# Attention with normalised queries and keys, then an MLP: later starts of three preparation units and a reordered list of first operations

## The chip, the cores and the metric

The kernel runs on one core of a Trainium2 chip. The metric is the device time of one execution in microseconds. Before the change it is 615.18 us, the median of three runs (614.29 to 615.19). The profiled execution took 614.88 us, and its trace spans 613.1 us; times inside the trace are counted from its start.

## The reference

What is computed, for 8 batches, 12 heads, 448 positions and head size 64 (model width 768, hidden width 3072):

```python
q_n, k_n = (rmsnorm(q, g_q), rmsnorm(k, g_k))
scores = scale * np.matmul(q_n, k_n.transpose(0, 1, 3, 2))
scores = scores - np.max(scores, axis=-1, keepdims=True)
attn = np.exp(scores)
attn = attn / (np.sum(attn, axis=-1, keepdims=True) + 1e-09)
x = np.matmul(attn, v)            # heads side by side: (8, 448, 768)
xn = (x - mu) / np.sqrt(var + 1e-06) * g_ln
out = x + np.maximum(xn @ w_ch1, 0.0) @ w_ch2
```

## The kernel before

**Units and pairs.** Two heads make a pair; there are 48 pairs, six to a batch. The data is prepared in units: units 0 and 1 hold one pair each (pairs 0 and 1), all others two. Batch 0 is units 0 to 3, unit 4 is pairs 6 and 7, unit 5 pairs 8 and 9, unit 6 pairs 10 and 11, unit 7 pairs 12 and 13, unit 8 pairs 14 and 15, unit 9 pairs 16 and 17.

**Preparation.** `pieces` (L188) makes the small operations of a unit, each named by a letter: b takes the buffers, a and c are the squares of keys and queries on ACT (ScalarE), d and e their sums on DVE (VectorE), g the inverse roots on ACT, i the keys times the gains (DVE for units 0 and 1, else POOL), j and k the high and low 16-bit half of the keys (j on ACT or POOL, k on DVE), l the scaled queries on DVE, m a second copy of them, v, w and z the values' casts on POOL. The buffers of a unit, `qn` and `khl`, come from a pool that holds two of each (L86), so that a unit can only start to write when an earlier unit's tile has been read for the last time.

**Transposes.** Up to unit 7 the keys and queries of pair p are transposed on the tensor engine (PE): K p (`trans_k`, L308) and Q p (`trans_q`, L320). From pair 6 on both write the one PSUM tile `tr`, which DVE copies out (L318, L335). From unit 8 on (`DMA_UNIT`) the DMA transposes them: pieces x and y (L253, L265), issued by SP.

**Attention.** S p.i (`scores`, L339) is one product of 128 keys with 448 queries on PE and the exponential of it on ACT; two PSUM buffers `psS` hold the products until ACT has read them. V p.i (`values`, L361) multiplies with the values on PE; after V p.6 DVE divides and writes x (`evac_o`, L387). A pair has seven S and seven V. T p (`stats`, L531) takes statistics for the LayerNorm on DVE.

**LayerNorm and MLP.** For batch 0, A, N0 to N2 (DVE), X0 to X2 (transposes on PE, copied out by ACT, ACT and DVE; X0 and X2 use `tr`) and R (ACT) form the LayerNorm; U0 to U2 (`up_first`, L659) are the first three hidden column blocks of the MLP, one token tile each. M is a small maximum on DVE. The rest of the MLP is `mlp_chunks` (L610): up (L621, followed by a ReLU on ACT) and down (L637), the latter in groups of six products, first for columns 0 to 383 and then for 384 to 767 in batch 0.

**What sets the order.** The first attention, up to the first MLP, follows the list `ORDER` token by token, on all engines. L n loads a unit (SP), G loads the LayerNorm gains, G2 scales them, W n loads a third of the first MLP matrix (POOL's queue). From there on `attention` (L458) makes a list of steps, seven for each pair: step 7p+i holds S p.i, V of the pair before, K of pair p+1 at i = 2 and Q of pair p+1 at i = 4. Into these steps it places the pieces of the units 5 and up: the first ones (b, a, i) at step st, the last of the main pieces at step e, the others evenly between:

```python
st = max(7 * (p - 2 - m) + 2, last + 1, 7 * nb0)
e = max(7 * (p - 2) - 1, st + 5)
st, e = EARLY.get(u, (st, e))
...
at = st + (e - st) * x // (k - 1) if x < k else e + 1 + x - k
```

So `EARLY` overrides start and end for the units named in it. Without it, unit 7 has the steps 58 to 69, unit 8 72 to 83, unit 9 86 to 97. The two halves of the second MLP matrix are loaded with the first pieces of units 6 and 7 (L482, issued by POOL). `run_rest` (L698) interleaves: after each piece of the MLP of batch b it emits as many steps of the attention of batch b+1 as its share of the MLP's cost allows. The steps up to 90 fall into the MLP of batch 0; its last 13 pieces are emitted after them, around the LayerNorm of batch 1. In the list `ORDER` the order on each engine is the one written; in `run_rest` that holds for all engines but DVE, whose order is planned when the program is built.

Of the kernel before, what the change touches and what calls it, by code (L numbers as in the profile page):

```python
# [33 lines left out]


ORDER = """
G b0 a0 c0 L4 L5 i0 j0 e0 k0 gq0 l0 b1 m0 a1 c1 K0 Q0 d0 gk0 S0.0 S0.1 i1 e1 d1 g1 j1 l1 m1 z0
k1 b2 a2 S0.2 d2 c2 S0.3 S0.4 K1 V0.0 e2 i2 S0.5 Q1 g2 l2 S0.6 S1.0 j2 V0.1 S1.1 S1.2 m2 b3
V0.2 a3 V0.3 k2 c3 S1.3 K2 V0.4 S1.4 z2 V0.5 Q2 V0.6 V1.0 S1.5 i3 W0 d3 e3 S1.6 V1.1 V1.2 S2.0
j3 T0 V1.3 S2.1 S2.2 Q3 V1.4 S2.3 K3 S2.4 V1.5 V1.6 S2.5 g3 z3 S2.6 V2.0 S3.0 S3.1 V2.1 k3  # L40
S3.2 b4 V2.2 l3 S3.3 V2.3 m3 S3.4 a4 V2.4 K4 Q4 S3.5 V2.5 V2.6 S3.6 Q5 S4.0 V3.0 S4.1 V3.1
V3.2 d4 i4 K5 W1 c4 W2 V3.3 V3.4 V3.5 V3.6 S4.2 S4.3 V4.0 S4.4 S4.5 V4.1 e4 j4 T1 S4.6 S5.0 k4
g4 V4.2 V4.3 V4.4 V4.5 S5.1 l4 S5.2 S5.3 K6 V4.6 S5.4 z4 m4 b5 V5.0 S5.5 V5.1 G2 L6 V5.2 S5.6
V5.3 V5.4 V5.5 Q6 a5 i5 V5.6 T3 T4 S6.0 S6.1 S6.2 S6.3 T5 S6.4 A V6.0 V6.1 N0 V6.2 N1 V6.3
S6.5 S6.6 V6.4 X0 X1 U0 N2 d5 j5 R X2 K7 Q7 c5 e5 g5 k5 z5 l5 L7 V6.5 U1 U2 M m5 V6.6
""".split()
DMA_UNIT = 8
PE_SET = (DMA_UNIT + 1) % 2
EARLY = {5: (42, 49), 6: (47, 56)}
LN_EXP_SET = 6  # L50
UP_FIRST = 3
REC_LO, REC_HI = 1.0 / 3.0e7, 0.5
# [23 lines left out]
class _Fast:  # L76
# [381 lines left out]
    def attention(self):  # L458
# [3 lines left out]
        for u in range(4, nu):  # L462
            p, m = UNIT_PAIR[u], UNITS[u][2]
# [3 lines that stand above are left out]
            pieces = ["bai", "d", "c", "e", "j", "gv", "k", "l", "m", "w", "x", "y"]  # L467
# [469 lines left out]
```

## Time and profile before

| | value |
|---|---|
| time, median of 3 | 615.18 us (614.29 to 615.19) |
| span of the trace | 613.1 us |
| bytes moved by DMA | 75.29 MB, mean 123 GB/s |
| one exponential (128 x 448, L358) | 635 ns, 336 times |
| one up product (128 x 384 or 512 columns, L621) | 353 ns, 1134 times |
| one down product (L637) | 324 ns, 1368 times |

The profile gives for each engine how long it was busy, and the trace gives each instruction with its start and duration and, in brackets, how long the engine had been idle before it and what released it. A matmul's end is modelled, so neighbouring products overlap on paper; the distance from start to start is the better measure. A wait on several things is put down to the one that came last. "DMA share" is the mean busy share of the 16 DMA engines; in some stretches it exceeds 1. "PEld" is the weight load of the tensor engine, which runs beside its products.

### The profile page before, as it was taken

How to read it: one execution, taken by the hardware profiler on the slowest of the kernel's cores; microseconds unless marked ns; L12 is line 12 of the kernel's file. 1: busy time of each engine (PE TensorE's matmuls, PEld its weight loads, DVE VectorE, ACT ScalarE, POOL GpSimd, SP SyncE). 2: the span in 40 equal slices, each digit the busy share in tenths (PEclk: the TensorE clock that was granted, in tenths of full speed). 3: DMA queues.
4: the chain of work that ended last, by engine and by line, in shares of the span. 5: the costliest groups of instructions: out<-in, count | busy, mean ns of one | idle time of the engine just before them, and what ended most of it. 6: DMA issues, size and time to landing. Idle time of an engine off the chain costs nothing.

```text
span 613.1 us, 11532 instructions
## 1 busy us (share of the span) xinstructions
PE 580.8 (95%) x4500; PEld 346.3 (56%) x4500; DVE 286.8 (47%) x618; ACT 361.4 (59%) x697; POOL 188.2 (31%) x245
## 2 busy tenths in 40 slices
PE   2887999799999999999999999999999999999995
PEld 1555566455566666655566666655566666654564
DVE  5898566633356356643346355642355422440011
ACT  5996986338754498538755398537765377214200
POOL 2852621223452245514453145605322000000000
PEclk9999999899999999999999999999999999999999
DMA  9999999275766477847665496838523330030011
GB/s 193 272 212 207 213 221 189 31 222 134 122 109 128 117 123 150 180 106 144 105 108 141 107 136 151 176 104 151 119 59 87 91 61 2 27 104 0 1 52 56
DMA packets 130861, 75.29 MB, mean 123 GB/s; under 512 B 96656, under 2 KB 121040, under 8 KB 130800
## 3 DMA queue, kind: packets, MB, share of 16 engines
q1 hardware_dynamic: 114048, 45.12, 37.5%
q0 software_dynamic: 16080, 28.94, 21.1%
q8 instruction: 37, 0.61, 0.4%
q10 hardware_dynamic: 672, 0.43, 0.2%
q14 instruction: 24, 0.20, 0.1%
HBM read 52.36 MB, written 11.01 MB: 103 GB/s over the span
## 4 chain that ended last, share of the span: by engine, by line
PE 82%; DVE 2%; DMA 2%; ACT 2%; issue 1%; SPq 1%; DVEq 0%; ACTq 0%
PE psC L637 34%; PE psH L621 33%; PE psS L352 7%; PE oA L381 4%; PE oB L383 2%; PE psS L355 1%; PE psS L356 1%; DMA qkv<-in_k_dram 1%; DMA kU<-khl 1%; ACT E L358 1%; ACT qn L215 0%; DVE qn L67 0%; DVE stat L545 0%; DVE khl L240 0%; ACT khl L215 0%
## 5 line engine op out<-in xcount | busy, mean ns | idle before, releaser
L621 PE MATMUL psH<-xnT,w 128*128 128x512 f16 (+1 forms) x1134 | 241.9, 353 | 0.3 <-ACT hT L671 0.3
L637 PE MATMUL psC<-w,hT 128*128 128x384 f16 (+1 forms) x1368 | 235.6, 324 | 0.0
L358 ACT ACTIVATE E<-psS,rr_all 128x448 f16<-128x448 f32 x336 | 206.9, 635 | 47.8 <-PE psS L352 42.6
L623 ACT ACTIVATE hT<-psH 128x512 f16<-128x512 f32 (+1 forms) x189 | 104.1, 551 | 124.4 <-PE psH L621 121.6
L637 PEld LDWEIGHTS <-hT 128*128 128x128 f16 x1368 | 128.1, 98 | 74.8 <-issue 0.7
L621 PEld LDWEIGHTS <-w 128*128 128x128 f16 x1134 | 102.7, 98 | 81.2 <-issue 0.8
L352 PE MATMUL psS<-qU,kU 128*128 128x448 f16 x288 | 100.9, 358 | 10.9 <-ACT E L358 8.9
L381 PEld LDWEIGHTS <-E 128*128 128x128 f16 x1008 | 70.9, 98 | 51.0 <-issue 7.0
L229 POOL TENSOR_TENSOR qkv<-qkv,gprod 128x896 f32<-128x896 f32 x21 | 43.7, 2079 | 99.4 <-ACT khl L215 60.5
L381 PE MATMUL oA<-v,E 128*128 128x65 f16 x864 | 66.9, 194 | 0.1
L641 DVE SCALAR_TENSOR_TENSOR x<-psC,rs_all,x 128x384 f32<-128x384 f32 x48 | 28.9, 615 | 71.7 <-PE psC L637 71.2
L396 DVE RECIPROCAL rec_all<-oA 128x6 f32<-128x6 f32 x48 | 9.3, 194 | 96.6 <-PE oA L381 96.4
L383 PE MATMUL oB<-v,E 128*128 128x65 f16 x288 | 51.9, 194 | 0.1
L127 POOL DMA_DIRECT2D qkv<-in_k_dram x14 | 11.2, 797 | 129.7 <-ACT E L358 67.9
L218 DVE TENSOR_REDUCE ssq<-khl 128x14 f32<-128x896 f32 (+1 forms) x24 | 25.6, 1065 | 48.7 <-ACT khl L215 48.6
L352 PEld LDWEIGHTS <-kU 128*128 128x128 f16 x288 | 28.3, 99 | 24.6 <-issue 6.2
L218 DVE TENSOR_REDUCE ssq<-qn 128x14 f32<-128x896 f32 (+1 forms) x25 | 26.2, 1047 | 25.1 <-ACT qn L215 25.1
L67 DVE SCALAR_TENSOR_TENSOR qn<-qkv,rq 128x256 f16<-128x256 f32 (+1 forms) x72 | 26.5, 424 | 18.0 <-ACT rq L223 17.9
L383 PEld LDWEIGHTS <-E 128*128 128x128 f16 x336 | 32.5, 97 | 0.3 <-DVE xl L403 0.2
L398 DVE TENSOR_TENSOR x<-oA,rec_all 128x384 f32<-128x384 f32 x48 | 26.8, 558 | 1.5
L545 DVE BATCH_NORM_STATS2 stat<-x 128x6 f32<-128x256 f32 (+1 forms) x75 | 26.3, 405 | 0.7
L240 DVE TENSOR_TENSOR khl<-qkv,khl 128x896 f16<-128x896 f32 x21 | 22.8, 1087 | 7.1 <-ACT khl L237 6.3
(104 smaller groups left out, 446.7 us busy)
## 6 DMA issues: line engine op xcount, KB each, us to landing
out_dram<-x SPq DMA_DIRECT2D x20, 384.0 KB, 2.5
qkv<-in_k_dram POOLq DMA_DIRECT2D x14, 384.0 KB, 3.8
qkv<-in_q_dram POOLq DMA_DIRECT2D x14, 384.0 KB, 5.4
qkv<-in_v_dram POOLq DMA_DIRECT2D x14, 384.0 KB, 6.5
w<-in_moe_w_ch_dram POOLq DMA_DIRECT2D x3, 1536.0 KB, 14.5
w<-in_moe_w_ch_dram POOLq DMA_DIRECT2D x2, 2304.0 KB, 27.0
qkv<-in_k_dram SPq DMA_DIRECT2D x7, 384.0 KB, 5.7
qkv<-in_q_dram SPq DMA_DIRECT2D x7, 384.0 KB, 5.1
```

Of the source, the lines that this page charges most:

```text
L67: nc.vector.scalar_tensor_tensor(out=out, in0=x, scalar=8.0, in1=r.unsqueeze(2).broadcast_to([x.shape[0], g, D]), op0=ALU.mult, op1=ALU.mult)
L218: nc.vector.tensor_reduce(out=c["ssq"][:, n], in_=c["sq", n], axis=AX.X, op=ALU.add)
L229: (nc.vector if u in DVE_KG else nc.gpsimd).tensor_tensor(out=c["t"][1], in0=c["t"][1], in1=sh.gprod.unsqueeze(1).broadcast_to([128, g, D] ...
L352: nc.tensor.matmul(ps[:, 0:S], c["main"][:, ts(i, 128)], q[:, ts(h, S)], start=True, stop=True)
L358: nc.scalar.activation(out=c["E"][:, i], in_=ps[:, 0:S], func=AFT.Exp, scale=self.rr[:, g:g + 1], bias=EXP_BIAS)
L381: nc.tensor.matmul(oA[:, t, cs], E[:, i, ts(t, 128)], rhs, start=(i == 0 and t == 0), stop=(i == 6 and t == 2))
L383: nc.tensor.matmul(oB[:, cs], E[:, i, 320:448], rhs, start=(i == 0), stop=(i == 6))
L398: nc.vector.tensor_tensor(out=x[:, :, 128 * hp:128 * hp + 128].rearrange("p t (e d) -> p t e d", e=2), in0=oA[:, :, :, 0:D], in1=rec[:, 0: ...
L621: nc.tensor.matmul(ps[:, 0:N], sh.w1[:, dc, ts(f, 128)], xnT[:, dc, 0:N], start=(dc == 0), stop=(dc == NDC - 1))
L623: nc.scalar.activation(out=hT[:, f, 0:N], in_=ps[:, 0:N], func=AFT.Relu)
L637: nc.tensor.matmul(ps[:, 0:g[1]], hT[:, f, ts(t, 128)], sh.w2[:, f, cols], start=(f == 0), stop=(f == NFF - 1))
L641: nc.vector.scalar_tensor_tensor(out=x[:, cols], in0=ps[:, 0:g[1]], scalar=self.rs[:, b, t:t + 1], in1=x[:, cols], op0=ALU.mult, op1=ALU.add)
```

## The change

The change touches two constants. In `EARLY`, units 7, 8 and 9 start three steps later and end where they did. In `ORDER`, no operation is added or removed; some change places. It is meant to begin a unit only when the older buffers are no longer read, and to fill waits in the passage from the first attention to the first MLP.

```diff
 ORDER = """
-G b0 a0 c0 L4 L5 i0 j0 e0 k0 gq0 l0 b1 m0 a1 c1 K0 Q0 d0 gk0 S0.0 S0.1 i1 e1 d1 g1 j1 l1 m1 z0
-k1 b2 a2 S0.2 d2 c2 S0.3 S0.4 K1 V0.0 e2 i2 S0.5 Q1 g2 l2 S0.6 S1.0 j2 V0.1 S1.1 S1.2 m2 b3
-V0.2 a3 V0.3 k2 c3 S1.3 K2 V0.4 S1.4 z2 V0.5 Q2 V0.6 V1.0 S1.5 i3 W0 d3 e3 S1.6 V1.1 V1.2 S2.0
+b0 a0 c0 L4 i0 j0 e0 k0 gq0 l0 b1 m0 a1 c1 K0 Q0 d0 G gk0 S0.0 S0.1 d1 e1 L5 i1 g1 j1 l1 k1 m1
+z0 b2 a2 S0.2 d2 c2 S0.3 S0.4 K1 V0.0 e2 i2 S0.5 Q1 g2 l2 S0.6 S1.0 j2 V0.1 S1.1 S1.2 m2 b3
+V0.2 a3 V0.3 k2 c3 S1.3 K2 V0.4 S1.4 z2 V0.5 Q2 S1.5 V0.6 V1.0 i3 W0 d3 e3 S1.6 V1.1 V1.2 S2.0
 j3 T0 V1.3 S2.1 S2.2 Q3 V1.4 S2.3 K3 S2.4 V1.5 V1.6 S2.5 g3 z3 S2.6 V2.0 S3.0 S3.1 V2.1 k3
-S3.2 b4 V2.2 l3 S3.3 V2.3 m3 S3.4 a4 V2.4 K4 Q4 S3.5 V2.5 V2.6 S3.6 Q5 S4.0 V3.0 S4.1 V3.1
-V3.2 d4 i4 K5 W1 c4 W2 V3.3 V3.4 V3.5 V3.6 S4.2 S4.3 V4.0 S4.4 S4.5 V4.1 e4 j4 T1 S4.6 S5.0 k4
-g4 V4.2 V4.3 V4.4 V4.5 S5.1 l4 S5.2 S5.3 K6 V4.6 S5.4 z4 m4 b5 V5.0 S5.5 V5.1 G2 L6 V5.2 S5.6
+S3.2 b4 S3.3 V2.2 l3 a4 V2.3 m3 S3.4 V2.4 K4 S3.5 Q4 V2.5 V2.6 S3.6 Q5 S4.0 V3.0 S4.1 V3.1 i4
+V3.2 d4 T1 K5 V3.3 W1 c4 V3.4 V3.5 S4.2 S4.3 V3.6 S4.4 S4.5 W2 e4 V4.0 V4.1 j4 S4.6 S5.0 k4
+S5.1 g4 V4.2 l4 S5.2 V4.3 V4.4 V4.5 S5.3 K6 V4.6 z4 V5.0 S5.4 m4 b5 V5.1 G2 S5.5 L6 V5.2 S5.6
 V5.3 V5.4 V5.5 Q6 a5 i5 V5.6 T3 T4 S6.0 S6.1 S6.2 S6.3 T5 S6.4 A V6.0 V6.1 N0 V6.2 N1 V6.3
-S6.5 S6.6 V6.4 X0 X1 U0 N2 d5 j5 R X2 K7 Q7 c5 e5 g5 k5 z5 l5 L7 V6.5 U1 U2 M m5 V6.6
+S6.5 S6.6 d5 V6.4 X0 X1 U0 N2 R Q7 X2 c5 e5 j5 g5 k5 l5 z5 U1 U2 V6.5 M m5 V6.6 L7 K7
 """.split()
 DMA_UNIT = 8
 PE_SET = (DMA_UNIT + 1) % 2
-EARLY = {5: (42, 49), 6: (47, 56)}
+EARLY = {5: (42, 49), 6: (47, 56), 7: (61, 69), 8: (75, 83), 9: (89, 97)}
```

## The prediction

> **What bounds the kernel now.** I read the summary by engine first, then a table of stretches, to see where TensorE (PE) is not busy.
>
> ```profile
> span 613.1 us, 11532 instructions
> PE 580.8 (95%) x4500; PEld 346.3 (56%) x4500; DVE 286.8 (47%) x618; ACT 361.4 (59%) x697; POOL 188.2 (31%) x245
> ```
> ```profile
> 20.00:40.00 20.00, 16.77 (x217) 11.23 (x217) 18.46 (x35) 19.72 (x38) 14.15 (x18) 1.00 0.99 230
> 40.00:50.00 10.00, 7.04 (x83) 4.15 (x82) 9.59 (x28) 8.68 (x18) 5.11 (x3) 1.00 1.12 217
> 50.00:60.00 10.00, 7.21 (x102) 5.93 (x100) 8.22 (x13) 4.60 (x13) 2.22 (x4) 1.00 0.98 221
> 107.00:116.00 9.00, 5.62 (x39) 3.37 (x36) 3.37 (x5) 4.38 (x7) 2.73 (x2) 0.81 0.41 36
> 116.00:607.00 491.00, 490.64 (x3600) 287.11 (x3598) 204.74 (x457) 272.38 (x522) 140.11 (x189) 1.00 0.50 105
> ```
>
> The columns are stretch, length, busy time of PE, weight load, DVE, ACT and POOL, then granted clock, DMA share and GB/s. From 116 us on PE lacks 0.4 us in 491: whatever is saved before 116 reaches the end undiminished, and nothing can be saved after it. Before 116 there are three regions: the first attention to 50, where ACT (19.72 of 20) and DVE (18.46, later 9.59 of 10) are full; the passage to the first MLP, 50 to 60, with 2.8 us of idle PE; and a hole at 107 to 116, with 3.4 us of idle PE and a clock of 0.81. The timeline shows the hole:
>
> ```profile
> 106.17 0.22 PE L313 MATMUL tr<-id,khl 128*128 128x128 f16 x1
> 109.17 0.95 ACT L215 ACTIVATE khl<-qkv 128x896 f32<-128x896 f32 x1 [3.70 <-DMA kU<-khl]
> 110.16 1.09 DVE L218 TENSOR_REDUCE ssq<-khl 128x14 f32<-128x896 f32 x1 [4.89 <-ACT khl L215]
> 110.70 0.35 PE L352 MATMUL psS<-qU,kU 128*128 128x448 f16 x1 [2.68 <-ACT E L358]
> 111.16 0.65 DVE L318 COPY kU<-tr 128x960 f16<-128x960 f16 x1
> 111.86 0.27 PE L327 MATMUL tr<-id,qn 128*128 128x128 f16 x1 [0.69 <-DVE kU L318]
> ```
>
> The square of unit 9's keys (a9, L215) sits in ACT's queue at step 86 and waits 3.70 us, until unit 8's key transposes by DMA land (109.07). Behind it stand the exponentials of pair 12, whose scores were ready at 106.2 and 106.9; both psS buffers are full, so PE stops. On DVE the reduce of that square (d9) stands ahead of the copy of pair 13's keys (L318), so the query transposes wait 0.69 us more. Afterwards the clock is low: 0.66 from 111 to 116.
>
> The same wait, small, is visible at the other units: a7 started at 72.41, just as K9's transposes ended (72.37), a8 at 89.10 after K11's (89.07). Each begins at the step where the last reader of the older key buffer (two under the tag) is listed. The passage:
>
> ```profile
> 53.57 0.56 DVE L608 COPY xnT<-tr 128x768 f16<-128x768 f16 x1 [0.47 <-PE tr L600]
> 54.19 0.22 PE L313 MATMUL tr<-id,khl 128*128 128x128 f16 x1 [0.72 <-DVE xnT L608]
> 54.77 0.66 DVE L318 COPY kU<-tr 128x960 f16<-128x960 f16 x1 [0.64 <-PE tr L316]
> 55.48 0.22 PE L327 MATMUL tr<-id,qn 128*128 128x128 f16 x1 [0.75 <-DVE kU L318]
> ```
>
> X2, K7 and Q7 share one PSUM buffer, tr. PE waits for each DVE copy before it may fill tr again (0.72 and 0.75), with U1 queued behind.
>
> **What the Trainium skill says.** "PSUM — Partial Sum Buffer", section Engine vs sequencer instructions: "ScalarE/VectorE/GpSimdE queues are strict FIFO." The trace agrees: exponentials with scores from 106.2 start at 110.03, after the square. "TensorE: Matmul & The Clock Gate", section Why this matters for your kernels: PE gaps beyond about 3 us put the array back to half clock. Here a gap of 2.7 us and 0.7 us more is followed by the 0.66, and six 384-column products take 2.12 us instead of 1.14. "DMA: Bandwidth & Descriptors", section Issuing engines are not separate DMA queues: all queues interleave on the same 16 engines. The trace agrees: the DMA share is above 1.2 from 68 to 107, with two queues active.
>
> **The change, part by part.**
>
> 1. *Start of units 7, 8, 9 at steps 61, 75, 89 instead of 58, 72, 86, ends unchanged.* By the list of pieces, a9 and d9 move to step 89, c9 to 90; e9 and later come after the first MLP. K13 stays at step 86, Q13 at 88. Now a9 is listed after both, so unit 7's buffers are free. If the program still gives unit 9 those of unit 8, a9 waits until about 110.4, but only two scores of batch 1 are left, and PE has a psS buffer for each.
> Price without the hole: after the products at 106.88 (0.97 to the next start), PE has left before the 13 uninterrupted groups of products of the tail: one score 0.19, values 0.12, Q13 0.36, six products 0.97, score 0.19, values 0.12, last score 0.38, last values 0.25, together 2.6 us, so the tail starts at 107.85 + 2.6 = 110.45 instead of 115.76. Exponentials of 0.63 us keep up: S12.4's is done at 108.85, before S12.6 needs its buffer. **5.3 us**, all on PE's path, including the slow clock.
> For units 7 and 8 the late start removes ACT's small holds; PE waits of 0.28 us (76.89) and 0.27 (93.58) for exponentials stand right behind c7 and c8. I take **0.3** of 0.55.
> The pieces are squeezed: unit 8's low half of the keys (k8) goes from step 79 to 80, so its transposes issue at about 99.4 instead of 98.1; first needed at step 98, far away. Cost nothing: PE's scores of batch 1 hide it.
>
> 2. *W2's second half, issued with a7.* POOL's issue moves from 75.52 to about 78.4 (three steps of 1.2 us, less part 3's gain). It took 30.0 us to land; 108.4 if again 30. First used as the 13th down group, at 111.4 before part 3's gain, some 110.5 after it. Hidden, by 2 us. The DMA engines are saturated either way, so the last byte should come earlier than 108.4, since the other transfers finish sooner.
>
> 3. *Q7 between U0 and X2; K7 last; d5 ahead of N2.* Chain after: N1 ends on DVE at 51.2, d5 (1.08) 52.2, N2 (0.95) 53.2. PE does U0 to 53.0, then Q7 at once (tr is free since 51.6) to 53.5. DVE copies Q7 (0.62) to 54.25, X2's transposes (0.5) end 54.8, X2's copy (0.56) 55.5. U1 (1.04) runs behind it meanwhile from 54.75, U2 ends 56.9 (before: 58.0), V6.5, V6.6 and K7 take 1.0. The MLP starts at 57.9 instead of 58.73: **0.8 us**. K7's copy is last on DVE, behind e5, k5, l5 and the evacuation of pair 6, done near 61.2; S7.0 comes at 60.8, so it may wait 0.4. ACT's exponential behind it was bound by ACT itself (9.5 of 10 busy), which moves earlier with e5 by 1.1, so I keep 0.8 as the likely value and 0.3 as the low end.
>
> 4. *First attention: scores ahead of values, T1 and a4 earlier, g4 later.* ACT has 0.28 us of idle from 20 to 40; then it has a hold of 0.63 at 42.71, for S5.4 behind K6. With g4 after S5.1 the exponential of S5.3 fills it. DVE, however, is then the chain (V4.6's evacuation to 44.54, Q6's copy at 44.73), which gives back only **0.2**.
> T1 ahead of K5's copy (36.67) puts that at 37.7 to 38.3, still before S5.0 (38.82). e4 is 1.1 later, where g4 now stands.
>
> 5. *The rest costs nothing.* d1 before i1: g1 waits for ACT (13.50), not for d1 (12.77). G and L4 change places on SP: issued within 16 to 23 us, their data is first used by a4 at 32.6 and by G2 at 43.68. The moves of W1, W2, k1, m1, z0, j5 and z5 leave the order on their own engine as it was; V and S change places elsewhere within ACT's full stretch.
>
> Sum: 5.3 + 0.3 + 0.8 + 0.2 = 6.6; 615.18 − 6.6 = **608.6 us**.
>
> **The rivals.**
>
> *The hole moves to batch 1's LayerNorm.* Its last transpose issued at 124.0 and landed 2.6 later; psH starts at 128.43: 1.8 us of slack. d9 (1.09) now falls beside the evacuation of V11.6, and DVE's order after the first MLP's start is planned when the program is built. If both reduces (2 x 1.09, and a wait of some 3 us for c9) go ahead, the excess of 2.4 us and a slow clock of about 1 us cost 3.4: **612.0**. For it: d9 stood ahead of a needed copy before. Against: one reduce alone fits into the slack.
>
> *Only the passage or only the hole improves.* If another wait of the same size arises behind units 7 or 8, say a squeezed piece ahead of a pair copy on DVE, half of part 1 is lost: **611.3**.
>
> *W2 late, slower.* If the later issue and the load of unit 9 stretch it from 30 to 38 us, the 13th group starts at 117 instead of 110.5, and the slow clock adds 1.5: 608.6 + 8 = **616.6**. Against: the engines' bytes are unchanged and their queue is never empty from 68 to 107.
>
> **How the numbers follow.** Main case 0.75; LayerNorm 0.1; half lost 0.1; slower 0.05. Main's bounds: part 3 at 0.3, parts 1 (small) and 4 at nothing, 609.6; all idle of 0.5 to 1 us more removed, 607.6. Two in ten may fall out: the range 607.3 to 612.0 takes in the first two rivals but for their tails. Faster by over 0.2%: 0.93; same 0.02; slower 0.05.
>
> **What would show it.** In the profile after: a9 with no wait, or one that no PE wait follows; no PE wait over 1 us after 60; granted clock 1.00 from 60 on; the 13 uninterrupted down groups starting near 109.3; Q7 directly after U0, the first psH near 57.7; psC waiting for no transfer. Wrong if: PE waits at the second psC half (part 2), at the first psH of batch 1 (LayerNorm), or if the exponentials before 110 still queue behind a9.

## The result and the profile after

The kernel after takes 608.03 us (median of 4 runs, 607.63 to 608.46); the kernel before, beside it, 615.18 us (4 runs, 614.29 to 615.63). The ratio is 0.9886, with a 95% interval of 0.9868 to 0.9903: 7.15 us less. The forecast was 608.6 in a range of 607.3 to 612.0.

From the page of the kernel after, its head, the busy times by engine, and the chain that ended last, by engine:

```profile
span 605.9 us, 11525 instructions
PE 578.3 (95%) x4500; PEld 344.6 (57%) x4500; DVE 286.5 (47%) x618; ACT 360.7 (60%) x697; POOL 189.5 (31%) x245
PE 88%; DVE 1%; ACT 1%; issue 0%
```

The span is 7.2 us shorter; the engines' busy times have hardly moved (PE 580.8 to 578.3, of which the hole's slow clock is a part). So what went was idle time: PE's share of the chain that ended last rose from 82% to 88%. The table of stretches, with the columns of the one before (the stretches fit the new times of the stages):

```profile
50.00:60.00 10.00, 8.22 (x110) 6.70 (x109) 8.76 (x16) 5.94 (x15) 2.86 (x4) 1.00 0.93 212
80.00:100.00 20.00, 20.00 (x198) 13.31 (x196) 14.22 (x29) 16.05 (x35) 4.46 (x5) 1.00 1.33 225
100.00:108.00 8.00, 8.00 (x81) 5.41 (x80) 3.84 (x10) 5.04 (x9) 0.09 (x1) 1.00 0.60 96
108.00:110.00 2.00, 2.00 (x19) 1.24 (x15) 1.91 (x5) 0.61 (x1) 2.00 (x2) 1.00 0.40 82
110.00:600.00 490.00, 489.40 (x3592) 285.81 (x3590) 205.11 (x455) 272.85 (x523) 140.70 (x189) 1.00 0.52 106
```

From 80 to 110 PE is busy for the whole stretch at a clock of 1.00; the hole is gone, and with it the 0.81. From 50 to 60 its idle time is 1.8 us instead of 2.8. Between 60 and the tail two of PE's old waits, 0.28 us at 76.89 and 0.27 at 93.58, are gone. The timeline where the hole was:

```profile
106.22 0.22 PE L327 MATMUL tr<-id,qn 128*128 128x128 f16 x1
106.84 0.94 ACT L215 ACTIVATE khl<-qkv 128x896 f32<-128x896 f32 x1
107.59 0.35 PE L352 MATMUL psS<-qU,kU 128*128 128x448 f16 x1
107.81 1.09 DVE L218 TENSOR_REDUCE ssq<-khl 128x14 f32<-128x896 f32 x1 [0.37 <-ACT khl L215]
108.50 12.84 PE L637 MATMUL psC<-w,hT 128*128 128x384 f16 x78
111.79 0.95 ACT L215 ACTIVATE qn<-qkv 128x896 f32<-128x896 f32 x1 [3.17 <-DVE stat L560]
```

The square of unit 9's keys (106.84) runs with no idle time before it: unit 8's key transposes had landed by then, the last at 106.06. Two exponentials are behind it, and PE needs neither before the tail ends. The 78 products of the tail, 13 groups of six, start at 108.50 instead of 115.76. The square of the queries (111.79) does still come after 3.17 us of idle time (the line names the signal that came last, DVE's; unit 8's last query transpose landed just before it, at 111.72), but of what stands behind it PE wants nothing before the tail ends. The passage to the MLP:

```profile
52.92 0.22 PE L327 MATMUL tr<-id,qn 128*128 128x128 f16 x1
53.58 0.62 DVE L335 COPY qU<-tr 128x896 f16<-128x896 f16 x1 [0.52 <-PE tr L330]
54.26 0.49 PE L600 MATMUL tr<-id,xn 128*128 128x128 f16 x6 [0.79 <-DVE qU L335]
54.59 2.17 PE L667 MATMUL psU<-xnT,w 128*128 128x128 f16 x36
57.38 3.08 PE L621 MATMUL psH<-xnT,w 128*128 128x384 f16 x18
60.93 0.55 PE L352 MATMUL psS<-qU,kU 128*128 128x448 f16 x2 [0.46 <-DVE kU L318]
```

Q7 fills PE right after U0, one wait for a DVE copy remains (0.79) where two stood in a row, and the MLP begins at 57.38. In return the first score of pair 7 waits 0.46 us for K7's copy.

**Where the 7.2 us lie.** I marked the same instructions in the PE timeline of every kernel and took the differences between their starts: K0 (first key transposes), X0 (first LayerNorm transposes), the first psH of the MLP, the first and the tenth group of psC, the tail of 13 groups, and the end of the last psC. All in us, from the profiled executions; the runs are explained below.

| kernel | K0 at | K0 to X0 | X0 to psH | psH to psC | psC to tenth | tenth to tail | tail to end | X0 to tail |
|---|---|---|---|---|---|---|---|---|
| before | 9.03 | 40.75 | 8.95 | 33.13 | 15.02 | 8.88 | 491.12 | 65.98 |
| after | 8.49 | 41.24 | 7.65 | 32.87 | 14.69 | 3.56 | 491.14 | 58.77 |
| e1_early_only | 8.89 | 41.83 | 8.95 | 32.86 | 14.70 | 3.56 | 491.13 | 60.07 |
| e2_order_only | 10.04 | 41.29 | 7.65 | 33.13 | 15.01 | 6.85 | 491.13 | 62.64 |
| e3_unit9_only | 9.01 | 41.83 | 8.95 | 33.12 | 15.02 | 3.56 | 491.14 | 60.65 |
| e4_units78_only | 9.46 | 40.76 | 8.94 | 32.88 | 14.70 | 8.71 | 491.12 | 65.23 |
| e6_unit9_at_87 | 8.86 | 40.75 | 8.95 | 33.12 | 15.02 | 4.80 | 493.28 | 61.89 |
| e6b_other_buffers | 9.12 | 41.94 | 8.94 | 33.12 | 15.02 | 3.56 | 491.14 | 60.64 |
| e7_k7_ahead | 8.86 | 41.26 | 7.65 | 32.86 | 14.70 | 3.56 | 491.14 | 58.77 |
| e8_warm | 9.08 | 41.27 | 7.65 | 32.87 | 14.70 | 3.56 | 491.14 | 58.78 |
| e9_warm_longer | 8.98 | 43.23 | 7.65 | 32.87 | 14.70 | 3.56 | 491.14 | 58.78 |
| e10_warm_held | 8.89 | 40.98 | 7.65 | 32.86 | 14.69 | 3.57 | 491.13 | 58.77 |
| e11_v06_ahead | 10.09 | 41.95 | 7.65 | 32.88 | 14.70 | 3.56 | 491.14 | 58.79 |
| e12_old_front | 9.79 | 40.73 | 7.65 | 32.87 | 14.70 | 3.56 | 491.14 | 58.78 |

Before to after: the hole 8.88 − 3.56 = 5.32, of which 3.37 were PE's two waits (2.68 and 0.69 in the prediction's timeline) and the rest mostly slow products; the stretches beside units 7 and 8, 0.26 + 0.33 = 0.59; the passage 1.30; together 7.21. The first attention is 0.49 longer, and K0 came 0.54 earlier in this execution (with the first list of before it varies from 8.86 to 9.79, with that of after from 8.49 to 10.09, so that counts as chance). The MLP after the tail is the same to 0.02: what is saved before it reaches the end.

Two things blur the times of single runs and not this table from X0 on: the start of K0, and a first attention that takes 40.7 or 41.9 us with the very same list (last section). So I read small effects from the table, which has one execution of each kernel, and large ones from both. One of the twelve executions of e2_order_only took 2157.4 us, and its ratio below leaves it out.

### The profile page after: what moved, and what is told of

It reads as the page before. It is cut to its first block, busy times and chain, and to the rows that moved or that the text cites. A ratio compares the mean times of both kernels' runs of the same rounds, so it can differ in the third digit from the quotient of the medians.

```text
span 605.9 us, 11525 instructions
## 1 busy us (share of the span) xinstructions
PE 578.3 (95%) x4500; PEld 344.6 (57%) x4500; DVE 286.5 (47%) x618; ACT 360.7 (60%) x697; POOL 189.5 (31%) x245
## 4 chain that ended last, share of the span: by engine, by line
PE 88%; DVE 1%; ACT 1%; issue 0%
PE psC L637 36%; PE psH L621 34%; PE psS L352 8%; PE oA L381 5%; PE oB L383 2%; PE psS L356 1%; PE psS L355 1%; PE tr L330 0%; PE tr L316 0%; ACT E L358 0%; DVE x L398 0%; DVE qn L67 0%; DVE khl L240 0%; ACT khl L215 0%; ACT hT L623 0%
## 5 line engine op out<-in xcount | busy, mean ns | idle before, releaser
L352 PEld LDWEIGHTS <-kU 128*128 128x128 f16 x288 | 28.0, 98 | 25.5 <-issue 6.0
## 6 DMA issues: line engine op xcount, KB each, us to landing
w<-in_moe_w_ch_dram POOLq DMA_DIRECT2D x2, 2304.0 KB, 24.3
```

Of the source, the lines that this page charges most:

```text
L352: nc.tensor.matmul(ps[:, 0:S], c["main"][:, ts(i, 128)], q[:, ts(h, S)], start=True, stop=True)
```

## The experiments

My theory: the hole came from a9 waiting, at the head of ACT's queue, for unit 8's key transposes by DMA; only unit 9's start removes it, the order list gives the passage, and nothing moves elsewhere. Rivals: the hole needs the list too, or moves elsewhere.

### The two constants apart

```diff
 # e1_early_only: the list of before, with
-EARLY = {5: (42, 49), 6: (47, 56)}
+EARLY = {5: (42, 49), 6: (47, 56), 7: (61, 69), 8: (75, 83), 9: (89, 97)}
 # e2_order_only: the list of after, EARLY of before
```

> Only the starts of units 7, 8 and 9 move; the list of the first attention is the old one. Theory (the hole at 107 to 116 is unit 9's square waiting in ACT's queue for unit 8's key transposes, and later starts free it): the 5.3 us of the hole and the 1.2 us between S7.0 and the hole go, the 0.7 us of the passage stays: 615.2 - 6.5 = 608.7. Rival (the earlier passage is what lets the later steps run without waits): well under half of the gain, 612 or more.

> Only the list of the first attention is new; the starts of units 7, 8 and 9 are the old ones. Theory: the passage's gain, 0.7 us at S7.0, arrives at the hole, whose length is set by two engines that both move earlier: 614.5. Rival (unit 8's transposes are held by the DMA traffic and land at 109 whatever PE does, so the hole swallows what the passage gains): 615.2, with a hole longer by 0.7 us.

Measured: e1 609.59 us (ratio 0.9908, 0.9887 to 0.9929), e2 614.13 us (0.9986, 0.9972 to 1.0001). From X0 to the tail `EARLY` alone gains 5.91 us, which with the passage's 1.30 is exactly the 7.21 of both. e1 was expected at 608.7: its theory counted 1.2 us for the stretches beside units 7 and 8, which gave 0.59, and the profiled execution had the long first attention besides, 1.08 over that of before. The list alone gains 3.34 in that stretch in its profiled execution (613.19 us): its passage, and 2.03 of the hole, since a9 at 108.56 waited 2.84 us there instead of 3.70. Less of that shows in the time, since this execution's K0 came 1.01 later and its first attention took 0.54 longer. So even with `EARLY` as before, the size of the hole is a race between PE's progress and the DMA; how it varies from execution to execution, one trace cannot show.

### Which unit

```diff
 # e3_unit9_only, on the kernel before
-EARLY = {5: (42, 49), 6: (47, 56)}
+EARLY = {5: (42, 49), 6: (47, 56), 9: (89, 97)}
 # e4_units78_only, on the kernel before
-EARLY = {5: (42, 49), 6: (47, 56)}
+EARLY = {5: (42, 49), 6: (47, 56), 7: (61, 69), 8: (75, 83)}
```

> Only unit 9 begins three steps later; units 7 and 8 and the list are the old ones. Theory: the hole alone goes, 615.2 - 5.3 = 609.9. Rival (the square merely moves its wait to step 89, where it still holds ACT, as unit 8's transposes land at 109.1 here): a hole of 1 to 2 us stays, 611 to 612.

> Only units 7 and 8 begin three steps later; unit 9 begins at step 86 as before. Theory: the waits of about 1.2 us between 61 and 107 go; unit 8's key transposes land near 106 as they do with the whole change, while PE reaches step 86 only 1.2 us earlier, so the hole shrinks from 5.3 us to 2 to 4 us: 612 to 614. Rival (the start of unit 9 is all that counts): 615.2.

Measured: e3 610.39 us (0.9921, 0.9898 to 0.9943), e4 615.77 us (1.0012, 0.9999 to 1.0025). In e3 the hole is gone (3.56), with the stretches beside units 7 and 8 as before. ACT's two squares of unit 9 in e3, from its timeline:

```profile
110.10 0.95 ACT L215 ACTIVATE khl<-qkv 128x896 f32<-128x896 f32 x1 [0.17 <-DMA kU<-khl]
113.94 0.95 ACT L215 ACTIVATE qn<-qkv 128x896 f32<-128x896 f32 x1 [2.34 <-DMA qU<-qn]
```

The wait is still in the program and is named by its releaser, the DMA's read of `khl`; three steps later it lasts 0.17 us. e4 missed my 612 to 614. The two stretches gained 0.25 and 0.32, but the hole stayed at 8.71, and now two squares are in PE's way (ACT and PE lines of e4, the scores behind the squares, and six products between):

```profile
108.51 0.95 ACT L215 ACTIVATE khl<-qkv 128x896 f32<-128x896 f32 x1 [3.17 <-DMA kU<-khl]
110.03 0.35 PE L352 MATMUL psS<-qU,kU 128*128 128x448 f16 x1 [2.16 <-ACT E L358]
111.58 1.14 PE L637 MATMUL psC<-w,hT 128*128 128x384 f16 x6
113.32 0.95 ACT L215 ACTIVATE qn<-qkv 128x896 f32<-128x896 f32 x1 [2.82 <-DMA qU<-qn]
114.85 0.35 PE L355 MATMUL psS<-qU,kU 128*128 128x448 f16 x1 [1.82 <-ACT E L358]
```

I had reckoned that unit 8's later start would move its transposes clear of a9. It moves them the wrong way: the first is issued at 99.18 here (98.10 before), as part 1 of the prediction said of k8, and PE arrives earlier by the 0.6 gained; the first square waits 0.53 less than before, the second 1.13 more. The six products between take 1.14 us, where they took 2.12 in the kernel before: the hole is as long without a slow clock, so the slow clock is not its cause. In this trace the stretch from X0 to the tail is 0.75 shorter than before, which the times do not show (615.77 us, against 615.41 for the kernel before beside it). Whether units 7 and 8 alone are worth anything stays open; beside unit 9's move they are worth 0.58 (e1 against e3 in the table).

### The cause: buffers or steps

Unit 9 at step 87, one step later than the kernel before has it, once with the buffers that the pool gives it and once with those of unit 7, whose readers are PE's transposes:

```diff
 # e6_unit9_at_87, on the kernel before
-EARLY = {5: (42, 49), 6: (47, 56)}
+EARLY = {5: (42, 49), 6: (47, 56), 9: (87, 97)}
 # e6b_other_buffers: the same, and in begin()
+            if u == 9:
+                c["qn"], c["khl"], _ = self.units[7]
+            else:
                 c["qn"] = self.p_n.tile(...)
                 c["khl"] = self.p_n.tile(...)
```

> The kernel before, with unit 9 at steps 87 to 97 instead of 86 to 97: one step later, still in the buffers of unit 8, as the built program shows for every version so far. Theory (the square waits for unit 8's key transposes to land, near 109): the square arrives at 107.5, waits about 1.5 us, and the exponentials of two scores more are ahead of it; a hole of 1 to 3 us of the 5.3 stays: 611.5 to 613. Rival (only the order of the reduce and the pair copy on DVE counts): any start after 86 is as good as 89, 610.

> As the run before, unit 9 at steps 87 to 97, but unit 9 takes over the two tiles of unit 7 instead of those of unit 8; order and work are the same. Theory: the square and the squares of the queries wait only for the last transposes of pair 13 on the tensor engine, which are listed before them; no hole: 610. Rival (placement or DMA traffic, not the buffer, makes the hole): the same time as the run before.

Measured: e6 613.56 us (0.997, 0.9955 to 0.9984), just over the 611.5 to 613; e6b 611.07 us (0.9926, 0.9907 to 0.9946), with a long first attention in the profiled execution (+1.19 on e6), without which it would be 610. From the timeline of e6b (its lines are 3 further down), ACT's squares of unit 9 and the tail:

```profile
108.05 0.94 ACT L218 ACTIVATE khl<-qkv 128x896 f32<-128x896 f32 x1
110.04 0.94 ACT L218 ACTIVATE qn<-qkv 128x896 f32<-128x896 f32 x1
111.70 12.84 PE L640 MATMUL psC<-w,hT 128*128 128x384 f16 x78
```

At the same steps, with the buffers alone exchanged, neither square waits and the hole is gone: 3.56 against e6's 4.80. This settles the cause at step 87: unit 9 takes over unit 8's buffers, and the DMA's late read of them makes the hole. At step 86 the buffers cannot be exchanged in this way, since pair 13's transposes still read those of unit 7; there the cause is read from the same wait with the same releaser (3.70 us, DMA `kU<-khl`). From the timeline of e6, ACT, DVE and PE:

```profile
108.85 0.95 ACT L215 ACTIVATE khl<-qkv 128x896 f32<-128x896 f32 x1 [2.14 <-DMA kU<-khl]
113.91 1.09 DVE L218 TENSOR_REDUCE ssq<-qn 128x14 f32<-128x896 f32 x1 [2.46 <-ACT qn L215]
121.75 1.67 DVE L641 SCALAR_TENSOR_TENSOR x<-psC,rs_all,x 128x384 f32<-128x384 f32 x3
122.42 1.79 PE L637 MATMUL psC<-w,hT 128*128 128x384 f16 x10 [1.99 <-DVE x L641]
```

It also shows a part of my first rival: the reduces ahead on DVE. The reduce of the queries' squares (e9, 113.91) waits 2.46 us at the head of DVE's queue, ahead of the division of the last values, whose products ended at 111.66 and which started at 114.91; the evacuations of psC then come late, and PE waits 1.99 us inside the tail. In the table it is the 493.28 instead of 491.14. The rival had PE wait at the first psH of batch 1; here that one, at 126.32, does not wait. In the kernel after, the planned order of DVE puts e9 at 116.72, behind the LayerNorm's operations, and nothing waits for it.

### The new wait at S7.0

```diff
 # e7_k7_ahead, on the kernel after
-S6.5 S6.6 d5 V6.4 X0 X1 U0 N2 R Q7 X2 c5 e5 j5 g5 k5 l5 z5 U1 U2 V6.5 M m5 V6.6 L7 K7
+S6.5 S6.6 d5 V6.4 X0 X1 U0 N2 R Q7 X2 c5 e5 j5 g5 k5 l5 z5 U1 U2 V6.5 K7 M m5 V6.6 L7
```

> The whole change, with pair 7's key transposes and their copy one place earlier, ahead of the maximum, unit 5's query copy and pair 6's evacuation on DVE. It takes away the wait of 0.46 us of the first score of pair 7 (60.93). Theory (ACT's exponentials are the limit right after): the wait goes, and the first down group starts no earlier: 608.0. Rival: the 0.5 us arrives: 607.5.

Measured: 608.96 us (0.9895, 0.9876 to 0.9915). S7.0 comes 2.92 us after the first psH instead of 3.55 and waits no more. But from psH to psC it is 32.86, as in the kernel after (32.87). The wait has moved to the third score (PE timeline of e7):

```profile
62.79 0.35 PE L352 MATMUL psS<-qU,kU 128*128 128x448 f16 x1 [0.59 <-ACT E L358]
```

So the 0.46 cost nothing: ACT's exponentials set the pace there, whatever the copy of K7 does. The trace agrees with the theory; the time does not come below that of the kernel after.

### The tensor clock in the first attention

The first transposes run at a low clock. The kernel has a token H n: n products of 384 columns whose result nobody reads. I put them ahead of K0, with one operand zeroed.

```diff
 # e8_warm, on e7: 14 products first, their operand in `vl` (zeroed)
-b0 a0 c0 L4 i0 j0 e0 k0 gq0 l0 b1 m0 a1 c1 K0 Q0 d0 G gk0 S0.0 S0.1 d1 ...
+H14 b0 a0 c0 L4 i0 j0 e0 k0 gq0 l0 b1 m0 a1 c1 K0 Q0 d0 G gk0 S0.0 S0.1 d1 ...
 # e9_warm_longer, on e8
+H26 b0 a0 c0 L4 i0 j0 e0 k0 gq0 l0 b1 m0 a1 c1 K0 Q0 H5 d0 G gk0 S0.0 S0.1 H5 d1 ...
+z0 b2 a2 S0.2 d2 c2 H3 S0.3 ...
 # e10_warm_held, on e9
-z0 b2 a2 S0.2 d2 c2 H3 S0.3 ...
+z0 b2 a2 S0.2 d2 c2 S0.3 ...
```

> The version of the run before, with 14 products of 384 columns on the identity matrix and a zeroed tile into a spare PSUM buffer at the very start, whose result is not used. It asks whether the slow tensor clock of the first 11 us of work (transposes of 0.29 us instead of 0.22, scores of 0.53 instead of 0.35) costs anything. Theory: the first score starts 0.5 to 0.8 us sooner after the first transpose and ACT, which is full afterwards, passes it on: 607.3. Rival: ACT and DVE hide it, 608.0; or zeros do not raise the clock and the first products are late, 608.5.

> Edit, on the kernel of the run with the warm-up: 26 instead of 14 products ahead of the first transposes, so that TensorE is busy until about 9 us, and 5, 5 and 3 more behind Q0, S0.1 and c2, so that its gaps between 10 and 15 us are filled. Theory: the granted clock reaches full speed at about 6 us and holds, S0.0 takes 0.35 us instead of 0.53, and the first attention is shorter by the slow products and copies behind them, some 1 us: X0 minus K0 at 40.2 instead of 41.2, the time 607.3. Rival 1: the first attention is set by ScalarE's exponentials whatever the clock, so the time is that of the kernel after, 608.0 to 608.9. Rival 2: the extra products stand in front of the first scores and delay them: 609.5.

> Edit: the run before without its three products behind c2, which waited 3.43 us for GpSimd's write to their operand and held the scores behind them; the 26, 5 and 5 stay. Theory: full speed holds from 6 to 13 us, S0.0 comes 2.4 us after K0 instead of 2.7, and the clock stays up behind it: X0 minus K0 at 40.2 instead of 41.2, the time 607.5. Rival 1: the 0.5 us that the first exponential gains are taken back by the engines that are full behind it: X0 minus K0 at 41.2 and 608.0 to 608.9. Rival 2: the clock still falls at 16 us and stays low longer: X0 minus K0 at 42, 609.5.

Measured: e8 608.86 us (0.9893, 0.9874 to 0.9913), e9 610.26 us (0.992, 0.9904 to 0.9935), e10 610.09 us (0.991, 0.9891 to 0.993). All three missed the 607.3 to 607.5 of their theories. In e8 the 14 products took 4.46 us, and K0's six transposes 0.50 instead of 0.85 at low clock, but after the gap of 2.13 us ahead of K0 the clock was low again at Q0 (0.82 for six). e9 was spoilt by my own edit: its third group read `vl`, which GpSimd writes for unit 0, and waited 3.43 us with the scores behind it (PE timeline of e9):

```profile
16.38 0.81 PE L452 MATMUL psW<-vl,id 128*128 128x384 f16 x3 [3.43 <-POOL vl L291]
```

e10 without that group held the clock up to 15.8 us and brought S0.0 2.42 us after K0 instead of 2.78. By 16.13 a score took 0.53 again, and low clock lasted to 22.9. Of the 0.36 us, 0.26 reached X0 (40.98). Its median time does not show even that. In e10 PE waits for ACT's exponentials between 10 and 20 us (1.45 us ahead of the score at 14.77), and shorter products passed on 0.26 us at most: the products' own duration is hardly what bounds that part.

### The first attention's list

```diff
 # e11_v06_ahead, on the kernel after
-... z2 V0.5 Q2 S1.5 V0.6 V1.0 i3 W0 d3 e3 S1.6 ...
+... z2 V0.5 Q2 V0.6 V1.0 S1.5 i3 W0 d3 e3 S1.6 ...
 # e12_old_front, on the kernel after: all lines of the list of before, but for the last line
```

> Edit, on the kernel after: V0.6 and V1.0 stand ahead of S1.5 again, as in the list before. Background: the first attention, from the first key transposes (K0) to the first LayerNorm transposes (X0), takes 41.24 to 41.29 us in the runs with the new list, against 40.75 in those runs with the old list in which the transposes at 22 us are at full clock. In the trace after VectorE waits 0.31 us at 23.89 for V0.6, whose products stand behind S1.5, which waits 0.41 us for a free buffer; from there to X0 VectorE has hardly any idle time. Theory: that is where the 0.4 us come from; without it VectorE never waits there, X0 minus K0 is 40.85 and the time 607.6. Rival 1: the later moves (T1, g4, c4, W2) cost it, and X0 minus K0 stays at 41.25: 608.0. Rival 2: with V0.6 ahead the clock rises later, as in three runs with the old list: 41.8, 608.6.

> Edit, on the kernel after: the lines of the list before for the whole first attention, and only the last line (the passage to the MLP) and the later starts of units 7 to 9 as in the kernel after. Theory: part 4 and the small moves of the change gain nothing in the first attention: X0 minus K0 is 40.75 where the clock is up at 22 us, else 41.85, the passage 7.65, the time 607.5 or 608.6. Rival: the moves of T1, a4 and g4 gain the 0.2 us predicted, and this kernel is slower than the one before it in this group by 0.2.

Measured: e11 609.27 us (0.9893, 0.9874 to 0.9912), e12 608.87 us (0.9895, 0.9875 to 0.9915). Neither time can be told from that of the kernel after; in the profile e12's first attention takes 40.73 and that of after 41.24. Both have K2's transposes at full clock (six in 0.50), so the clocks are alike and the difference is the list's: the new one is 0.5 longer. Relative to K0 the two agree to 0.01 up to Q2 (13.88); then the first division of pair 0 starts 15.02 after K0 in e12 (24.81 − 9.79) and 15.40 in the kernel after (23.89 − 8.49). Timeline of the kernel after, PE's score S1.5 and DVE's division:

```profile
23.34 0.35 PE L352 MATMUL psS<-qU,kU 128*128 128x448 f16 x1 [0.41 <-ACT E L358]
23.89 0.20 DVE L396 RECIPROCAL rec_all<-oA 128x6 f32<-128x6 f32 x1 [0.31 <-PE oA L381]
```

and in e12 the copy of Q2 and the same division:

```profile
24.26 0.62 DVE L335 COPY qU<-psQ 128x896 f16<-128x896 f16 x1 [0.16 <-PE psQ L330]
24.81 0.18 DVE L396 RECIPROCAL rec_all<-oA 128x6 f32<-128x6 f32 x1
```

With S1.5 ahead of V0.6, PE waits at S1.5 for an exponential, V0.6 stands behind it, and DVE, which from the division to the LayerNorm shows only one more wait (0.30 us at 44.68), starts it 0.38 us later. e11 undoes just that. The wait of DVE is gone there, but its execution had the late clock, so the 0.4 could not be read off it: it came out at rival 2's number, 41.95. Against the executions with the old list and the late clock (41.83 to 41.94) it leaves 0.01 to 0.12 for all other moves, T1, a4 and g4 among them, and on the slower side. So no gain of these is seen; the 0.4 of S1.5 is read from the two traces and not shown by an experiment of its own. That the 0.2 of part 4 would make e12 the slower kernel is not borne out: its first attention is the shorter one.

## Why the prediction came out right, point by point

- **Part 1, the hole, 5.3.** Measured 5.32, shown by e3. The tail was forecast "near 109.3" and started at 108.50; from X0 it came 7.21 us earlier. What removed it is not the release that the text put first, "unit 7's buffers are free": even at step 89 the program gives unit 9 the buffers of unit 8 (e3 waits 0.17 us for the DMA's read), and a9's wait stays in it. The other branch that the text kept open is the one that holds, but milder: a9 was to wait until about 110.4 with nothing urgent behind it. In fact a9 started at 106.84 with no idle time: the last key transpose landed 4.3 us after its issue and not 6.0 as before, and why, no run separates. It is c9 that waits, 3.17 us, when PE has no scores left.
- **Units 7 and 8, 0.3 of 0.55.** Mis-sized: 0.59, of which 0.26 before the first psC and 0.33 up to the tenth. The prediction took about half of the waits without giving a reason; all of it came. With unit 9's move it is 0.58 (e1 against e3); what it is alone, e4 leaves open.
- **Part 2, W2 hidden.** Right. Its two loads took 24.3 us on the page after, 27.0 before. The second half, issued at 77.33, landed at 102.6, against 108.4 in the forecast; the 13th group, the first to need it, is the second of the tail and started at 109.48, with 6.8 us to spare.
- **Part 3, the passage, 0.8.** The chain went as written: Q7's copy ended at 54.20 (54.25 forecast), X2's transposes at 54.75 (54.8), X2's copy at 55.35 (55.5). The term was mis-sized behind it: U1 began at 54.59, U1 and U2 took 2.01 us instead of 2.15, V6.5, V6.6 and K7 0.78 instead of 1.0. So the MLP began at 57.38 and not at 57.9, and the passage gave 1.30. S7.0's "may wait 0.4" was 0.46 and cost nothing (e7). Keeping 0.3 as the low end for it was needless.
- **Part 4, first attention, 0.2.** Wrong: no gain of these moves is seen (e11 is 0.12 longer than e3), and 0.5 lost in all (after against e12). The failing step is in part 5: "V and S change places elsewhere within ACT's full stretch", at nothing. It looked at ACT alone, and by the two traces S1.5 ahead of V0.6 cost DVE some 0.4. Part 4 had itself named DVE as the chain.
- **The sum.** 5.3 + 0.3 + 0.8 + 0.2 = 6.6 was forecast; 5.32 + 0.59 + 1.30 − 0.49, and 0.54 by K0's chance start, make 7.26; the last psC ends 7.24 us earlier in the trace. That the total is so near is luck: two terms were 0.8 too small together, one was 0.7 too large and had the wrong sign, and the first attention could as well have been the long one.
- **Rivals.** The first (LayerNorm behind the reduces) did not occur with unit 9 at step 89, but it did at 87, at 2.14 us (e6), where 3.4 had been worked out, and inside the tail and not at the first psH. The second and the third did not occur.

## What to carry to other kernels

When a wait is removed by starting something later, ask which resource it waits for and whether the wait is gone or only no longer in the way: here the buffer's reader was a DMA, and a start three steps later merely let it finish, while one step was too little. An instruction that waits at the head of an in-order queue costs what is queued behind it, so place it where nothing urgent follows, and check all engines for each exchange of two operations: one that is free for the engine that looks full can stall the one that passes its result on. Compare distances between marks in the trace beside the total time; terms of half a microsecond that the runs' spread hides can be read from them.

## What the runs showed that I had not expected

The same instructions took 40.7 or 41.9 us in the first attention. With the old list up to X0, four executions (before, e4, e6, e12) lie within 40.73 to 40.76 and three (e1, e3, e6b) within 41.83 to 41.94. The parting comes before the transposes of Q2: in the first these run at full clock, in the others, and in e11, at low. In e3 and e11 the clock had not risen by then; in e1 and e6b scores took 0.35 us from 19 us on, and from 22 to 25.5 us the products were slow again. PE timelines of e12 and of e11, a score and Q2:

```profile
20.84 0.35 PE L352 MATMUL psS<-qU,kU 128*128 128x448 f16 x1 [0.24 <-ACT E L358]
23.73 0.50 PE L330 MATMUL psQ<-id,qn 128*128 128x128 f16 x6
```
```profile
24.10 0.56 PE L352 MATMUL psS<-qU,kU 128*128 128x448 f16 x1
24.78 0.85 PE L330 MATMUL psQ<-id,qn 128*128 128x128 f16 x6
```

DVE's copies then wait for them (that of Q2 0.90 us in e11 and 0.16 in e12), and as DVE is the full engine here (27.71 of the 30 us from 20 to 50 in the kernel after), the delay stays, about 1.1 us. The Trainium skill, "TensorE: Matmul & The Clock Gate", section Part 1: The HAM clock gate (the "warmup" mystery), says that the activity window of 3.4 us is free-running, so that the switch depends on where in it the work falls. The executions with the old list agree with it in kind, since nothing in the list differs up to there; where the window lay, the trace does not show. With the new list after, e2, e7 and e8 all had the early clock, 41.24 to 41.29. S1.5 ahead of V0.6 cannot have brought it: it starts at 23.34 in the kernel after, behind the point where the executions part, so that rival 2's number in e11 does not speak for rival 2. Whether the list's earlier moves make the early clock surer is open: e11 has them too and was late.

The column of the granted clock does not show this. Over 20 to 25 us it reads 1.00 both for e3, whose transposes took 0.85, and for the kernel after, with 0.50; for e1 it reads 0.72. At such places the durations tell the clock.
